# Zero-weight products with 64-row tiles and copies of dead banks, appended to the end of a one-core attention and feed-forward kernel

## The chip, the cores and the metric

The kernel runs on one core of a Trainium2 chip. The metric is device time in microseconds (us) of that core, the median of several executions. The profile is one more execution, in which the hardware profiler recorded every instruction of the core; its span runs from the first to the last instruction. PE is the matrix engine (PEld its weight loads), DVE the vector engine, ACT the scalar engine, POOL the third elementwise engine; SP issues most of the DMAs.

## What is computed

A gate mixes softmax attention with 32 heads of width 20 and a dense layer with the Mish activation, over 2048 rows of width 640. Cut to what matters:

```python
x = A_x                                             # [1, 2048, 640]
g = sigmoid((x * gate_w).sum(-1, keepdims=True))
q, k, v = split_heads(x @ A_wqkv)                   # 32 heads, 20 wide
a = concat_heads(softmax(q @ k.T * 20**-0.5) @ v) @ A_wo
h = x @ B_w1 + B_b1                                 # 1536 wide
b = (h * tanh(log1p(exp(h)))) @ B_w2
return g * a + (1 - g) * b
```

Both branches read the same input `A_x`. The appended work adds nothing to the output: it reads `xT` and a tile of zeros, writes accumulator banks whose last contents for the output have been read by then, and copies two of them to `accs`, which is not stored.

## The kernel before, in words

The accumulator memory `K.ps` has eight banks of 128 partitions x 512 float32. Banks 0 to 6 serve scores and dense products, bank 7 (`ACCB`) holds the sum of probabilities times values for one group of four heads and 512 queries. Every matrix product goes through the helper `mm` (L507), so one line stands for all of them; products that use a part of the array are told apart in the profile by a pair such as `128*32`, contraction rows times output columns:

- `32*128`, scores: each uses 32 rows of the array (one head, padded), and up to four with different rows run beside each other, each writing a bank of its own.
- `128*32`, values and dense layers: each uses 32 columns of the array. `mm4` (L512) issues four of them, for the four quarters of a bank's partitions; they run beside each other. Below, such a set of four is called a group. Some groups in the middle of the kernel have the tile of zeros, `K.zero`, as weights.

The order of all work was written down beforehand: a planner (`make_plan`) emits small functions, a stored list (`ORDER`) gives their order, and the last loop of the kernel calls them. Each engine then runs its own instructions strictly in that order; waits between engines are semaphores that the framework places where one instruction needs another's result. The last instructions of each engine are those of the output projection: on PE groups of 320 columns, on DVE `ost` (L751), on ACT `otmp` (L1218), on POOL the sum of the two (L1221), and on SP six stores of 128 rows each to the output (L452). Behind its last store SP waits for every DMA queue and every engine, and then the engines meet in a barrier (listed at the line of the last loop, L1801).

Lines that come up: L1394 and L1396 copy one half each (256 columns) of the last `ACCB` to `accs`, on DVE and on ACT; L1571 is a DVE copy on whose result PE's next weight load waits; L1753 are the 24 zero-weight products that open the program.

The banks in which PE's last groups ended, and that the output's last DVE and ACT instructions read, lie among 0 to 5; `ACCB` was read last near 735 us of the span.

Of the kernel before, what the change touches and what calls it, by code (L numbers as in the profile page):

```python
# [12 lines left out]
ACT = mybir.ActivationFunctionType  # L13
# [8 lines left out]
QC, NQC = 512, 4  # L22
# [6 lines left out]
NBANK, ACCB = 7, 7  # L29
# [232 lines left out]
def unpack(text):  # L262

    lo, out = 0, set()
    for k in range(0, len(text), 3):
        i = lo + int(text[k : k + 3], 16)
        yield i
        out.add(i)
        while lo in out:
            out.remove(lo)  # L270
            lo += 1
# [149 lines left out]

def make_plan(K, par):

# [25 lines left out]
    def ld(f):  # L449
        def fn():  # L450
            d, s = f()
            K.nc.sync.dma_start(out=d, in_=s)  # L452

        return fn

    def ldn(fs):
        def fn():
            for f in fs:
                d, s = f()
                K.nc.sync.dma_start(out=d, in_=s)  # L460

        return fn

    for (a, b), t in zip(XD, XAT):
        for i in range(a, b):
            pl.at(t, (lambda i=i: pl.give(("x", i))))
    pl.at(4300.0, lambda: act_q.append((460.0, (lambda: pad0(K.wk0, K.wkp)), (lambda: pl.give("wk0")))))
    pl.at(5600.0, lambda: act_q.append((460.0, (lambda: pad0(K.wq0, K.wqp)), (lambda: pl.give("wq0")))))
    pl.at(12200.0, lambda: pl.give("wv0"))
# [6 lines left out]
    def pad0(raw, dst):  # L476
        K.nc.scalar.activation(
            dst.rearrange("p k (r d) -> p k r d", r=4)[:, :, :, 0:DH], raw.rearrange("p k (r d) -> p k r d", r=4), ACT.Copy
        )
# [1172 lines left out]
    return dict(pl=pl, stat=stat, blk=blk, gtimes=gtimes, uinfo=uinfo)  # L1652


@with_exitstack
def kernel(
    ctx: ExitStack,
# [11 lines left out]
    nc = tc.nc  # L1669
    x2d = A_x[0]  # L1670
    K = Names()
    K.nc, K.A_wqkv, K.A_wo, K.B_w1, K.B_b1, K.B_w2 = nc, A_wqkv, A_wo, B_w1, B_b1, B_w2
    K.outp = out[0].rearrange("(p t) d -> t p d", t=NS)
    ctx.enter_context(tc.manual_schedule())
# [76 lines left out]
    for _ in range(NWARM):  # L1751
        for q in range(4):
            nc.tensor.matmul(  # L1753
                K.ps[32 * q : 32 * q + 32, ACCB, :],
                lhsT=K.zero,
                rhs=K.wkp.rearrange("p k c -> p (k c)")[:, 0:QC],
                start=True,
                stop=True,
                tile_position=(0, 32 * q),
                skip_group_check=True,  # L1760
# [12 lines left out]
    for i in unpack(ORDER):  # L1773
        for fn in plan["pl"].fns[i]:
            fn()


# [28 lines left out]
```

## Time and profile before

| what | us |
|---|---|
| executions | 746.64 and 747.2 |
| median | 746.92 |
| span of the profiled execution | 745.1 |
| busy: ACT / DVE / POOL | 713.2 / 607.1 / 521.9 |
| PE's share of the chain that ended last | 80% |

The profiled span is 1.8 us under the median of the timed executions. "Busy" is the time in which an engine had at least one instruction in flight. In a timeline each row is a run of equal instructions on one engine: the start, how long the run took, the engine, the line, what it writes and reads, and how many; a bracket says how long the engine had been idle and who released it. SPq, DVEq and the like are an engine's sequencer: its waits (EVENT_SEMAPHORE) and DMA issues. The granted clock of the matrix engine was 1.000 on average over the span.

### The profile page before, as it was taken

Reading aid. Unit: us, or ns where it says so; the run is one execution under the profiler, and the core shown is the slowest. Engines: PE = TensorE matmul, PEld = TensorE weight load, DVE = VectorE, ACT = ScalarE, POOL = GpSimd, SP = SyncE. Lnnn points to the kernel's source line nnn. Section 1 sums busy time; section 2 is a strip of 40 time slices with the busy share of each in tenths; the row PEclk is TensorE's granted clock in tenths of the full one; section 3 lists DMA queues with packets and bytes.
Section 4 is the critical chain, followed back from the end, with each engine's and each line's share of the span. In section 5 each row is a group of like instructions: output and inputs, shape, how many; then the busy total and the mean of one; then the engine's idle time right before and its main releaser. Section 6 shows DMA issues by size and latency. Waiting matters only on the chain.

```text
span 745.1 us, 24873 instructions
## 1 busy us (share of the span) xinstructions
PE 729.6 (98%) x10332; PEld 255.2 (34%) x10332; DVE 607.1 (81%) x1047; ACT 713.2 (96%) x750; POOL 521.9 (70%) x501
## 2 busy tenths in 40 slices
PE   8999999999999999999999999999999999999997
PEld 4433343333235333333332222223433333333333
DVE  4688888888979797988788878887878788797876
ACT  6899989999999999999999999999999999999995
POOL 9466735565578557667676587687986788797884
PEclk9999999999999999999999999999999999999999
DMA  9611120011011000112102211130111111211202
GB/s 284 199 48 54 50 82 17 20 52 39 17 29 60 16 29 26 50 44 74 39 28 59 54 43 50 39 101 21 43 52 39 39 38 39 71 60 60 72 21 86
DMA packets 45720, 41.82 MB, mean 56 GB/s; under 512 B 20120, under 2 KB 39240, under 8 KB 45608
## 3 DMA queue, kind: packets, MB, share of 16 engines
q1 hardware_dynamic: 42984, 39.94, 17.8%
q8 instruction: 80, 1.31, 0.7%
q10 hardware_dynamic: 2624, 0.31, 0.3%
q14 instruction: 32, 0.26, 0.1%
HBM read 27.59 MB, written 12.38 MB: 54 GB/s over the span
## 4 chain that ended last, share of the span: by engine, by line
PE 80%; ACT 10%; DVE 7%; issue 2%; POOL 0%; DVEq 0%; ACTq 0%; POOLq 0%
PE ps L507 80%; ACT E L1312 9%; DVE E L1347 4%; DVE E L1365 2%; DVE accs L1406 0%; POOL E L1365 0%; ACT act L1236 0%; PE ps L1753 0%; PE ps L520 0%; ACT xT L528 0%; ACT L1236 0%; DVE bst L656 0%; DVEq L1801 0%; DVE qT L544 0%; DVE ost L689 0%
## 5 line engine op out<-in xcount | busy, mean ns | idle before, releaser
L1312 ACT ACTIVATE E<-ps 128x1024 bf16<-128x1024 f32 (+2 forms) x723 | 680.0, 1070 | 19.3 <-PE ps L507 16.4
L1365 POOL TENSOR_SCALAR E<-E 128x1024 uint16<-128x1024 uint16 x431 | 457.8, 1063 | 209.7 <-DVE E L1347 155.0
L1347 DVE TENSOR_SCALAR E<-ps 128x512 uint16<-128x512 f32 x584 | 388.8, 684 | 94.1 <-PE ps L507 85.6
L507 PE MATMUL ps<-E,VA 128*32 128x512 bf16 x3216 | 299.4, 383 | 1.7 <-DVE E L1347 0.6
L507 PE MATMUL ps<-qT,kT 32*128 32x512 bf16 x2048 | 284.0, 384 | 5.3 <-ACT E L1312 2.6
L507 PEld LDWEIGHTS <-kT 32*128 32x128 bf16 x2048 | 75.3, 91 | 261.3 <-issue 257.2
L507 PEld LDWEIGHTS <-VA 128*32 128x32 bf16 x3216 | 78.9, 95 | 97.5 <-issue 78.2
L1365 DVE TENSOR_SCALAR E<-E 128x1024 uint16<-128x1024 uint16 x153 | 97.9, 643 | 2.0
L507 PE MATMUL ps<-R,act 128*32 128x320 bf16 x1536 | 87.1, 302 | 0.4 <-ACT act L1236 0.4
L507 PE MATMUL ps<-xT,R 128*32 128x512 bf16 x960 | 82.4, 383 | 0.0
L507 PEld LDWEIGHTS <-R 128*32 128x32 bf16 (+1 forms) x1728 | 40.8, 95 | 44.7 <-issue 34.0
L507 PEld LDWEIGHTS <-act 128*32 128x32 bf16 x1536 | 36.4, 95 | 32.1 <-issue 22.2
L637 DVE TENSOR_SCALAR act<-ps,b1f 128x512 bf16<-128x512 f32 x48 | 35.7, 744 | 7.4 <-PE ps L507 6.6
L507 PE MATMUL ps<-wv,xT 128*32 128x241 bf16 (+2 forms) x720 | 37.6, 276 | 0.5 <-DVE E L1347 0.3
L507 PE MATMUL ps<-wk,R 128*32 128x320 bf16 (+1 forms) x640 | 37.5, 303 | 0.2
L507 PE MATMUL ps<-xT,wq 128*32 128x512 bf16 x400 | 34.8, 383 | 0.1
L507 PE MATMUL ps<-xT,wk 128*32 128x512 bf16 (+1 forms) x360 | 34.7, 384 | 0.0
L1620 POOL TENSOR_TENSOR ons<-accs,rb 128x512 bf16<-128x512 f32 x24 | 31.5, 1310 | 1.8 <-DVE E L1347 0.7
L567 DVE CAST stg<-ps 128x512 bf16<-128x512 f32 (+1 forms) x40 | 27.3, 683 | 5.1 <-PE ps L507 4.9
L507 PEld LDWEIGHTS <-xT 128*32 128x32 bf16 (+1 forms) x720 | 19.6, 96 | 13.0 <-issue 9.4
L1406 DVE COPY accs<-ps 128x512 f32<-128x512 f32 x31 | 21.2, 684 | 1.3 <-PE ps L507 1.0
L1236 ACT ACTIVATE act<-act 128x3072 bf16<-128x3072 bf16 x8 | 21.5, 2752 | 0.0
(72 smaller groups left out, 190.3 us busy)
## 6 DMA issues: line engine op xcount, KB each, us to landing
rb<-rd_d SPq DMA_DIRECT2D x124, 64.0 KB
qd<-stg SPq DMA_DIRECT2D x20, 128.0 KB
b_d<-bst SPq DMA_DIRECT2D x16, 160.0 KB
out_dram<-ost SPq DMA_DIRECT2D x16, 160.0 KB
kT<-kd SPq DMA_DIRECT2D x28, 80.0 KB
qT<-qd SPq DMA_DIRECT2D x28, 80.0 KB
stg<-b_d SPq DMA_DIRECT2D x13, 160.0 KB
kd<-stg SPq DMA_DIRECT2D x16, 128.0 KB
```

Source lines behind the costliest of these rows:

```text
L507: K.nc.tensor.matmul(o, lhsT=l, rhs=r, start=first, stop=last, tile_position=pos, skip_group_check=True)
L567: K.nc.vector.tensor_copy(out=K.stg[0:w, s, :], in_=bank(b)[0:w, :])
L637: K.nc.vector.tensor_scalar(out=K.act[:, f, (c % 2) * QC : (c % 2 + 1) * QC], in0=bank(b), scalar1=K.b1f[:, f : f + 1], scalar2=None, op0= ...
L1236: K.nc.scalar.activation(a, a, ACT.Mish)
L1312: lambda: K.nc.scalar.activation(K.E[:, e : e + w, :], K.ps[:, b0 : b0 + w, :], ACT.Exp, scale=SCALE)
L1347: lambda: K.nc.vector.tensor_scalar(out=K.E[:, e + h, :].bitcast(U16), in0=K.ps[:, b, :], scalar1=CH_MUL, scalar2=CH_OFF + CH_ADD[0], op0= ...
L1365: eng.tensor_scalar(out=o, in0=i, scalar1=float(CH_ADD[k]), scalar2=1.0, op0=ALU.add, op1=ALU.mult)
L1406: emit(lambda: K.nc.vector.tensor_copy(out=K.accs[:, g % 2, :], in_=K.ps[:, ACCB, :]))
L1620: gp_q.append((1350.0, lambda: K.nc.gpsimd.tensor_tensor(out=dst(), in0=K.accs[:, b, :], in1=K.rb[:, b, :], op=ALU.mult), lambda: pl.give( ...
```

## The change

One function is added and called behind the loop that calls the planned functions, and a semaphore is allocated that nothing uses. The planned work and its order stay what they were on every engine.

`product` is one zero-weight product into a quarter of a bank. `full` is a group with all 128 rows of the array; `half(r, b)` is a group with 64 rows, the upper (`r` = 0) or the lower (`r` = 1), into bank `b`. `link` puts an empty instruction on an engine which waits for product `a`, and makes the products of list `b` wait for the empty instruction. `chain` writes the upper and the lower part of one sum into `ACCB` in turns, with a link at each turn and `more` pairs of half groups into other banks between the turns.

```diff
+def end_products(K):
+    dep = mybir.DependencyInfo(mybir.DependencyClass.Sync, mybir.DependencyReason.DATA)
+
+    def product(row, rows, col, b, n=QC, first=True, last=True):
+        return K.nc.tensor.matmul(
+            K.ps[32 * col : 32 * col + 32, b, 0:n],
+            lhsT=K.zero[row : row + rows, :],
+            rhs=K.xT[row : row + rows, 0, 0:n],
+            start=first,
+            stop=last,
+            tile_position=(row, 32 * col),
+            skip_group_check=True,
+        )
+
+    def full(b):
+        for q in range(4):
+            product(0, 128, q, b)
+
+    def half(r, b, n=QC, first=True, last=True):
+        return [product(64 * r, 64, q, b, n, first, last) for q in range(4)]
+
+    def link(eng, a, b):
+        n = eng.nop()
+        K.tc.add_manual_dep(n.ins, a.ins.name, dep, reason="row tiles in turn")
+        for i in b:
+            K.tc.add_manual_dep(i.ins, n.ins.name, dep, reason="row tiles in turn")
+
+    def chain(eng, more, b=None):
+        for k in range(4):
+            a = half(0, ACCB, first=True, last=False)
+            if b:
+                link(eng, b[-1], a)
+            for j in range(more):
+                half(0, (k + j) % 3)
+                half(1, 3 + (k + j) % 3)
+            b = half(1, ACCB, first=False, last=True)
+            link(eng, a[-1], b)
+            for j in range(more):
+                half(1, 3 + (k + j) % 3)
+                half(0, (k + j) % 3)
+        return b
+
+    full(ACCB)
+    full(ACCB)
+    b = chain(K.nc.sync, 1)
+    full(ACCB)
+    b = chain(K.nc.vector, 1, b)
+    full(ACCB)
+    chain(K.nc.sync, 2, b)
+    full(ACCB)
+    for _ in range(6):
+        half(0, 1)
+    half(1, 4)
+    K.nc.vector.tensor_copy(out=K.accs[:, 0, :], in_=K.ps[:, 4, :])
+    for _ in range(6):
+        half(0, 0)
+    full(ACCB)
+    for _ in range(6):
+        product(0, 64, 0, 0)
+    for q in range(1, 4):
+        product(0, 64, q, 0)
+    K.nc.vector.tensor_copy(out=K.accs[:, 1, :], in_=K.ps[:, 0, :])
+    full(ACCB)
+    full(ACCB)
+    for k in range(8):
+        if k >= 4:
+            K.nc.vector.nop()
+            K.nc.scalar.nop()
+        K.nc.vector.tensor_copy(out=K.accs[:, 0, 0:256], in_=K.ps[:, 0, 0:256])
+        K.nc.scalar.activation(K.accs[:, 1, :], K.ps[:, 1, :], ACT.Copy)
...
+    K.tc = tc
+    K.psem = tc.alloc_semaphore('psem')
...
         for fn in plan["pl"].fns[i]:
             fn()
+    end_products(K)
```

In the built program this is, behind the last instruction of each engine as it was: on PE 445 products, each with a weight load; on SP 15 empty instructions, behind its last store; on DVE 8 empty instructions and 10 copies; on ACT 8 copies. Each empty instruction is a wait for one count of PE's semaphore and an increment of a semaphore of its own; the first weight load of the linked group waits for that. The eight empty instructions of the last loop, which no dependency names, leave nothing in the program. Each of the eight DVE copies and the eight ACT copies of that loop waits for the one before it on its engine, since it overwrites the same part of `accs`; the first of ACT waits for the DVE copy into `accs[:, 1, :]`, and that one for the last of the nine products into bank 0. On PE two more waits are new: the first group into bank 3 waits for the last `ost` of DVE, and the first into bank 1 for the last `otmp` of ACT.

## The prediction

> **What bounds the end now.** Nothing moves before the appended work, so I read the end and the price of each piece. First the page's head, for the span against which the sum is made, and PE's load; next the timeline of the last microseconds, all engines, and with it the timeline from 733 us for SP's stores and the two accumulator copies.
>
> ```profile
> span 745.1 us, 24873 instructions
> PE 729.6 (98%) x10332; PEld 255.2 (34%) x10332; DVE 607.1 (81%) x1047; ACT 713.2 (96%) x750; POOL 521.9 (70%) x501
> ```
>
> ```profile
> 733.91 8.35 SPq L452 DMA_DIRECT2D out_dram<-ost  x6
> ...
> 734.34 0.43 DVE L1394 COPY accs<-ps 128x256 f32<-128x256 f32 x1 [0.45 <-PE ps L507]
> ...
> 734.80 0.38 ACT L1396 ACTIVATE accs<-ps 128x256 f32<-128x256 f32 x1 [1.16 <-DVE accs L1394]
> ```
>
> ```profile
> 740.33 0.32 PE L507 MATMUL ps<-wq,R 128*32 128x320 bf16 x4
> 740.33 0.53 ACT L1218 ACTIVATE otmp<-ps,gt 128x320 f32<-128x320 f32 x1 [1.58 <-PE ps L507]
> 740.40 1.47 DVE L751 SCALAR_TENSOR_TENSOR ost<-ps,gt,R 128x320 bf16<-128x320 f32 x3 [0.27 <-PE ps L507]
> 740.93 0.86 POOL L1221 TENSOR_TENSOR ost<-otmp,R 128x320 bf16<-128x320 f32 x1 [0.94 <-ACT otmp L1218]
> ```
>
> PE's last group starts at 740.33, DVE ends at 740.40 + 1.47 = 741.87, POOL at 741.79, SP issues its last store until 733.91 + 8.35 = 742.26. What follows to 745.1 is the landing of the stores and the closing barrier: 4.4 us in which PE does nothing. Appended work can hide there, and only there.
>
> Then prices. A stretch of PE's own timeline gives the step from group to group and what a change of the tile's form costs (first fence); a form-by-form list of ACT prices a copy (second); the timeline at 737.5 us (third) and the waits listed at two lines, count and shortest, median and longest ns (fourth), price a link.
>
> ```profile
> 722.28 0.60 PE L507 MATMUL ps<-E,VA 128*32 128x512 bf16 x8
> ...
> 724.84 0.31 PE L507 MATMUL ps<-wq,R 128*32 128x320 bf16 x4
> 725.08 0.39 PE L507 MATMUL ps<-qT,kT 32*128 32x512 bf16 x2
> 725.40 0.73 PE L507 MATMUL ps<-wk,R 128*32 128x320 bf16 x16
> ```
>
> ```profile
> L1312 ACT ACTIVATE E<-ps 128x1024 bf16<-128x1024 f32 x675 | 632.1, 1060 | 16.1 <-PE ps L507 13.4 <-POOL E L1365 0.5 <-ACT E L1312 0.3
> L1312 ACT ACTIVATE E<-ps 128x512 bf16<-128x512 f32 x15 | 9.4, 628 | 2.5 <-PE ps L507 2.4
> ```
>
> ```profile
> 737.50 0.29 DVE L1571 COPY R<-ps 128x256 bf16<-128x256 bf16 x1 [0.72 <-PE ps L1564]
> ...
> 737.85 0.12 PEld L507 LDWEIGHTS <-R 128*32 128x32 bf16 x8 [0.26 <-DVE R L1571]
> ```
>
> ```profile
> L452 SPq EVENT_SEMAPHORE  x26: 17/17/2224, 250.0 to 741.8; - x26
> ...
> L751 DVEq EVENT_SEMAPHORE  x4: 21/21/21, 737.5 to 740.4; - x4
> ```
>
> Readings. Two groups of 512 columns took 0.60 us where one takes 0.38: a step T = 0.22. Sixteen products of 320 columns took 0.73, so (0.73 - 0.31) / 3 = 0.14 a group, 34 ns a product with its weight load. From the 320-column group at 724.84 to the scores at 725.08 it is 0.24 instead of 0.14, and from the scores to the next form 0.32 instead of 0.22: a change of form costs s = 0.10. After the DVE copy ended at 737.79, PE's dependent load began at 737.85: 0.05 from engine to PE. PE's groups that ran from 739.91 for 0.44 ended at 740.35, and DVE began at 740.40: again 0.05. An empty wait takes 17 to 21 ns.
>
> **The sum, piece by piece.** A link starts at the end of a half group X, 0.39 after X's start (0.38 and the stagger of four), crosses to SP or DVE (0.05), waits there 0.02, crosses back (0.05): the linked group Y starts 0.51, with rounding 0.52, after X. In between PE streams one half group on X's side and one on the other. Four scores of different rows, into four banks, take 0.40 us in this trace (at 724.15), as long as one, so I take upper and lower half groups as running beside each other too: X and the pair need 2T = 0.44. The link ends last: P1 = 0.52 a turn. With `more` = 2 it is 3T = 0.66, over 0.52: the link is hidden and P2 = 0.66; if pairs ran faster, the link's 0.52 would be next late. `half` has a form of its own (64 rows), and the nearest row for its change is s = 0.10, between 128 and 32 rows; from below it is 0.
>
> The start: two full groups at 740.47 and 740.69, the first half group into `ACCB` at 741.01 (0.22 + s), bank 0 at 741.23. The group into bank 3 waits for DVE's 741.87. The first Y waits for SP's empty instruction, which stands behind the last store: 742.26 + 0.05 (issue to next, as SP does now) + 0.02 + 0.05, so 742.38. SP has nothing behind that but the other links and the closing waits; the store itself is not delayed. On DVE the links stand behind the last `ost`, and ahead of copies that need PE anyway. The waits for bank 1 (ACT, over at 740.86) and the landing stores cost nothing.
>
> - First chain: 6 more turns, 742.38 + 6 x 0.52 = 745.50. A step to the last pair, the full group after T + s, the next chain after T + s again: 0.22 + 0.32 + 0.32 brings it to 746.36.
> - Second chain, links on DVE: 7 x 0.52 + 0.86 = 4.50: 750.86.
> - Third chain: 7 x 0.66 + 2 x 0.22 + 0.32 + 0.32 = 5.70: 756.56.
> - Twelve half groups on one side, 12 x 0.22 = 2.64 (the one into bank 4 runs beside the sixth, and its DVE copy, 0.68 by the 512-column copies at L1406, hides under the next six): 759.20. Full group with two changes of form, 0.42: 759.62.
> - Six products on one and the same tile follow each other: the sixth starts 5 x 0.22 later, 760.72, the other three quarters beside it, end 761.12. The last two full groups, 0.6 us, hide under what follows.
> - The DVE copy of bank 0: 0.05 + 0.68, 761.85. From here the two engines run eight copies each. DVE: 0.43 by L1394, and 0.03 between an instruction and the next that needs it (L1554 behind L1553 at 735.99), 8 x 0.46 = 3.7. ACT: 256 columns took 0.38 and from 512 to 1024 it is (1060 - 628) / 2 = 216 ns per 256 columns, so 0.60, and 0.04 between dependent ones (an ACT instruction that waited for the one just before it began 43 ns behind it, at 630.5 us): 8 x 0.64 = 5.12. ACT ends last: 761.90 + 5.12 = 767.02. The eight empty instructions that would stand between copies are not in the program: nothing.
> - The closing: SP's last waits started at 743.84 and the span ended at 745.1, so 1.26 after its last wait; 0.03 to get there: 768.3.
>
> That is 23.2 us over 745.1. The profiled execution lies 1.8 under the median, and I let that stand: 746.92 + 23.2 = 770.1.
>
> **Bounds.** Below: a hidden link gives P1 = 0.44, 13 turns x 0.08 = 1.0; no cost of the form's change, eight on the path, 0.8; copies overlapping by 0.13, as ACT's independent instructions do (0.93 apart at 1.06 each), 8 x 0.17 = 1.3. Together 767.0. Above: a link dearer by 0.2 costs 13 x 0.2 and 7 x 0.06, 3.0: 773.1. The Trainium skill's page "TensorE: Matmul & The Clock Gate", section "The cost: per-tile semaphore tail", gives a formula for the time behind the last product, 70 ns for four tiles and one increment, an estimate where the trace has 50; by it the 13 binding links would cost 0.3 us more.
>
> **Rivals.**
>
> 1. *Upper and lower run one after the other.* The trace never shows 64-row tiles, nor eight tiles at once, only four. Then X and the pair take 3T = 0.66, with `more` = 2 five T = 1.10: 13 x 0.14 + 7 x 0.44 + about 1.1 for pairs at the chains' ends and the group into bank 4, 6.0: 776.1. For it: nothing but the absence of a row. Against: four row tiles of the scores together take 0.32 to the next form, as three do. 0.12.
> 2. *Links dearer by 0.2 or more*, an engine's sequencer slower to answer PE than to answer DVE: 773 to 776. Against: 17 and 21 ns waits at both. 0.06.
> 3. *A price per product at issue.* A P1 turn has 12 products, so it decides from 43 ns each, P2 from 33. The densest long rows show 34: P2 0.68, 0.1 us in all. The dearest row of short products is that of 128x80 at full array width, 4.8 us busy for 80, 60 ns each with their filling: P1 0.72, P2 1.20, 13 x 0.20 + 7 x 0.54 = 6.4, 776.5. Against: the 34 ns hold at the end of the kernel, over 16 products. 0.02. The Trainium skill's "TensorE: Matmul & The Clock Gate", section "Step-by-step: what each phase is for", has 62 ns a product where the sequencer decodes products in its firmware; by that rule, as an estimate, it would be 777, and the 34 ns measured here disagree with it.
> 4. *The clock falls.* The opening zero-weight products took 627 ns where later ones take 382. If the gaps of the chains lowered the clock, steps double: about 15 us, 785. Against: PE's longest gap would be some 0.8 us, at the start, and by the view of waits PE waited as long for ACT (L528) before; the mean granted clock was still 1.000. 0.03.
> 5. *Not slower.* The two halves share one accumulator bank; if a link did not hold PE's queue, and groups of the other side passed it, the three chains would be 44 pairs, 9.7 us, where I have 0.52 x 16 + 0.66 x 8 = 13.6. It decides where the whole addition falls to 14.9 us (2% of 746.92). Taking off 3.9, the lower bounds that this doesn't contain (0.8 and 1.3) and the wait at the start (0.9) leaves 16.3, 763.2; to reach 761.8 ACT's copies have to take 0.30 besides, where half their columns took 0.38. Against: each engine goes through its waits in order everywhere in this trace. 0.02.
>
> **The numbers.** The forecast itself, 767 to 773 around 770.1, has 0.75. The range takes in rival 1 and most of 2 and 3: 767 to 776.5. A measurement of this kernel tells 2% from no change, 14.9 us, and all cases but rival 5 lie over it: slower 0.97, within 2% 0.02, faster 0.01.
>
> **What would show it.** Right: in the trace after, turns of 0.52 us in the first two chains and 0.66 in the third; PE's last product near 761.5; eight ACT copies 0.64 apart and nothing after them but 1.3 us of barrier; all rows before 740 as they were. Wrong: lower half groups that start when upper ones end (rival 1); an idle gap on PE at each turn of the third chain too (2); 627-ns products (4). What would upset the sum most is a wait that I have not seen in the program's order: PE's queue held up by a load that waits while products behind it could run.

## The result

The changed kernel took 770.92 us, the median of 768.97 and 772.87, against 746.92 before: 1.0315 times as long, 95% interval 1.0248 to 1.0382. Forecast were 770.1 us and a range of 767.0 to 776.5. A second series, told below, gave 769.46 (six executions) against 746.86 (eleven), 1.0295 with an interval of 1.0264 to 1.0326.

The head of the page after:

```profile
span 771.0 us, 25807 instructions
...
PE 750.8 (97%) x10777; PEld 263.4 (34%) x10777; DVE 610.4 (79%) x1057; ACT 717.8 (93%) x758; POOL 522.1 (68%) x501
```

All 445 added products, 10 DVE copies and 8 ACT copies are there. But the span grew by 25.9 us, and not all of that is the change: this one execution was late before it came to the addition. The timeline of PE after shows where (start, length, engine, line, what, idle before):

```profile
5.47 1.28 PE L520 MATMUL ps<-ident,act 128*128 128x128 bf16 x10 [0.20 <-DMA act<-in_A_x_dram]
10.07 2.32 PE L507 MATMUL ps<-xT,wkp 128*32 128x512 bf16 x20 [3.32 <-ACT xT L528]
...
744.10 0.32 PE L507 MATMUL ps<-wq,R 128*32 128x320 bf16 x4
```

The same projection before, by PE's timeline:

```profile
7.23 1.26 PE L507 MATMUL ps<-xT,wkp 128*32 128x512 bf16 x20 [0.79 <-ACT xT L528]
```

PE waited 3.32 us for its first projection, and the granted clock averaged 0.81 between 7 and 16 us, where it had been 1.00 before; twenty products that had taken 1.26 us took 2.32. PE came to its last group of the output projection at 744.10 instead of 740.33. The next section tells whether this belongs to the change. The addition itself is read from that group on:

| from the start of PE's last projection group, us | forecast | after |
|---|---|---|
| first half group | 0.68 | 0.68 |
| first linked half group | 2.05 | 2.05 |
| second chain begins | 6.03 | 5.94 |
| third chain begins | 10.53 | 10.50 |
| the twelve half groups on one side begin | 16.23 | 15.33 |
| DVE copy of bank 0 | 20.84 | 19.89 |
| first ACT copy | 21.57 | 20.61 |
| last ACT copy ends | 26.69 | 25.61 |
| end of the span (before: 4.77) | 27.97 | 26.90 |

So the addition is 26.90 - 4.77 = 22.1 us, where 23.2 were forecast. One step is off by 0.9 us: from the beginning of the third chain to the twelve half groups it is 4.83 us, where 5.70 were forecast. The timeline of the weight loads shows the turns, since each linked group begins with a load that waits. First two turns linked by SP, then two by DVE, then the third chain:

```profile
746.15 0.13 PEld L1660 LDWEIGHTS <-zero 64*32 64x32 bf16 x12 [0.35 <-SPq L1678]
746.65 0.13 PEld L1660 LDWEIGHTS <-zero 64*32 64x32 bf16 x12 [0.37 <-SPq L1678]
...
750.57 0.13 PEld L1660 LDWEIGHTS <-zero 64*32 64x32 bf16 x12 [0.40 <-DVEq L1678]
751.09 0.13 PEld L1660 LDWEIGHTS <-zero 64*32 64x32 bf16 x12 [0.40 <-DVEq L1678]
...
755.10 0.33 PEld L1660 LDWEIGHTS <-zero 64*32 64x32 bf16 x20 [0.17 <-SPq L1678]
755.61 0.40 PEld L1660 LDWEIGHTS <-zero 64*32 64x32 bf16 x20 [0.17 <-SPq L1678]
756.18 0.33 PEld L1660 LDWEIGHTS <-zero 64*32 64x32 bf16 x20 [0.17 <-SPq L1678]
```

The turns are 0.50 us (SP) and 0.53 (DVE), forecast 0.52; but in the third chain 0.51 and 0.57 in turns, 0.54 on average, where the forecast had 0.66. The end of the chain of waits shows the rest, one copy after the other (start, length, what):

```profile
746.15 17.82 PE ps L1660 x414
763.97 0.02 issue
763.99 0.70 DVE accs L1717
764.69 0.02 issue
764.71 0.61 ACT accs L1725
765.32 0.02 issue
765.34 0.61 ACT accs L1725
...
769.11 0.60 ACT accs L1725
```

### The profile page after: what moved, and what is told of

It reads as the page before. It is cut to its first block, busy times and chain, and to the rows that moved or that the text cites. A ratio compares the mean times of both kernels' runs of the same rounds, so it can differ in the third digit from the quotient of the medians.

```text
span 771.0 us, 25807 instructions
## 1 busy us (share of the span) xinstructions
PE 750.8 (97%) x10777; PEld 263.4 (34%) x10777; DVE 610.4 (79%) x1057; ACT 717.8 (93%) x758; POOL 522.1 (68%) x501
## 4 chain that ended last, share of the span: by engine, by line
PE 80%; ACT 10%; DVE 7%; issue 2%; DMA 1%; POOL 0%; ACTq 0%; SPq 0%; DVEq 0%; POOLq 0%
PE ps L507 78%; ACT E L1312 8%; DVE E L1347 3%; PE ps L1660 2%; DVE E L1365 2%; DMA wq<-in_A_wqkv_dram 1%; ACT accs L1725 1%; DVE accs L1406 0%; POOL E L1365 0%; ACT act L1236 0%; ACT L1236 0%; DVE ost L751 0%; DVE bst L656 0%; DVE accs L1717 0%; DVE qT L544 0%
## 5 line engine op out<-in xcount | busy, mean ns | idle before, releaser
L1725 ACT ACTIVATE accs<-ps 128x512 f32<-128x512 f32 x8 | 4.8, 597 | 20.3 <-DVE accs L1717 20.1
```

Source lines behind the costliest of these rows:

```text
L1725: K.nc.scalar.activation(K.accs[:, 1, :], K.ps[:, 1, :], ACT.Copy)
```

## The experiments

My theory after this reading: the sum is right but for one step, that PE starts products strictly in the order of the program. Its rival keeps that order and looks for the 0.9 us elsewhere. T is the 0.216 us from group to group on one tile row.

**The same kernel again.** No edit.

> The changed kernel once more, five rounds. From PE's last product of the output projection to the end the first profile has 26.9 us, and 4.8 before, so the addition is 22.1 us and executions should lie at 746.9 + 22.1 = 769.0. The profiled execution was 3.8 us later already at the output projection. Theory 'chance': that comes from the order in which the first loads land, is no part of the change, and only some executions have it: most executions near 769.0, some near 772.9. Rival 'part of the change': every execution of the longer program starts late, all within 771 to 773.

Six executions: 768.46, 768.9, 769.28, 769.64, 769.8 and 771.92; median 769.46. Five lie within 0.8 us of 769.0 and one is late. The profiled one reached the last projection group at 740.51, and the seven other experiments, all with work added behind the same program, reached it between 739.67 and 741.56. The late start is no part of the change; it is in one of the first two executions, which is why their median is 0.8 us above the forecast though the addition was smaller. Its way is in the chain of waits of the first profile: the load of `wq` was issued at 1.22 us as in the other profiles, but ACT's copy of it, for which ACT's copy of `xT` and so PE had to wait, began at 8.89, where it began between 5.83 and 6.96 in the nine other profiles. Why the load was late is not shown. The kernel before has a late execution as well, one of its eleven with 753.35 us; that one and the 771.92 were not profiled, so whether they were late in the same way stays open.

In this profile the stretch from PE's last projection group to the end took 27.35 instead of 26.90, and the timeline shows the 0.45:

```profile
741.63 1.27 SPq L452 DMA_DIRECT2D out_dram<-ost  x2
...
743.00 0.13 PEld L1660 LDWEIGHTS <-zero 64*32 64x32 bf16 x12 [0.79 <-SPq L1678]
```

SP issued its last two stores until 742.90, 2.39 us after PE's last projection group at 740.51, instead of 1.94; the first linked group follows at 743.00. The first link does stand behind SP's stores.

**The copies left out.**

```diff
-    for k in range(8):
...
-        K.nc.vector.tensor_copy(out=K.accs[:, 0, 0:256], in_=K.ps[:, 0, 0:256])
-        K.nc.scalar.activation(K.accs[:, 1, :], K.ps[:, 1, :], ACT.Copy)
```

> Leaves out the last loop, the eight DVE and eight ACT copies. If they stand alone at the end, as the sum has it, the end comes with the DVE copy of bank 0, 0.68 us after PE's count: the stretch from PE's last product of the output projection to the end falls from 26.9 by 5.0 to 21.9 us, the time by 5.0 to about 764. Rival: the copies' place is taken by something else that ends late (the last two groups, the closing waits), and less than 4 us is gained.

764.39 us, 5.07 less than the 769.46; 1.0223 of before, interval 1.0191 to 1.0255. The stretch was 22.35, 5.00 less than the 27.35 of the run above; in both a last store took SP long to issue (0.74 and 0.79 us). The copies stand alone at the end, as the sum had it.

**The links left out.** The lower half groups write bank 6, so nothing has to be kept apart.

```diff
-            a = half(0, ACCB, first=True, last=False)
-            if b:
-                link(eng, b[-1], a)
+            a = half(0, ACCB)
...
-            b = half(1, ACCB, first=False, last=True)
-            link(eng, a[-1], b)
+            b = half(1, 6)
```

> The lower half groups of the chains write bank 6 instead of the shared bank, and the 23 empty instructions with their waits are gone; the same products stay. Theory 'passing' (a product whose tile is free starts ahead of older products that wait for another tile): both sides of the array stay full, a turn of three groups takes 1.5 T = 0.32 us instead of 0.50 (SP) and 0.53 (VectorE), the third chain stays at 2.5 T = 0.54; the addition falls by 8 x 0.18 + 8 x 0.20 + about 0.3 at the start = 3.3 us. Theory 'strict order' (of my prediction): a turn takes 2 T = 0.43, the addition falls by about 1.5 us.

766.67 us (four executions), 2.8 less than the 769.46. The loads of the three chains in its timeline:

```profile
743.16 2.27 PEld L1660 LDWEIGHTS <-zero 64*32 64x32 bf16 x87 [0.80 <-issue]
745.86 0.10 PEld L1660 LDWEIGHTS <-zero 128*32 128x32 bf16 x4 [0.43 <-issue]
746.19 2.30 PEld L1660 LDWEIGHTS <-zero 64*32 64x32 bf16 x96 [0.23 <-issue]
748.92 0.10 PEld L1660 LDWEIGHTS <-zero 128*32 128x32 bf16 x4 [0.42 <-issue]
749.25 4.03 PEld L1660 LDWEIGHTS <-zero 64*32 64x32 bf16 x160 [0.23 <-issue]
753.70 0.10 PEld L1660 LDWEIGHTS <-zero 128*32 128x32 bf16 x4 [0.43 <-issue]
```

From one full group's loads to the next, 745.86 to 748.92, is 3.06 us for the second chain's 24 half groups and the full group with two changes of form. That is (3.06 - 0.43) / 24 = 0.110 a half group, half of T: the two sides are both full. In strict order it would have been 8 x 0.43 + 0.43 = 3.9 and more. The third chain takes 753.70 - 748.92 = 4.78, and with the links it took 759.10 - 754.27 = 4.83: the links cost it 0.05 in all. From the last projection group to the twelve half groups it is 12.47 us (754.03 less 741.56), 2.86 less than the 15.33 of the first profile; "passing" had 3.3, "strict order" 1.5. Most of what "passing" had too much is in the first chain: its twelve lower groups all come after the wait for DVE's last `ost`, at 743.16 to 745.53, so one side alone takes 12 T there.

**How far a product passes.** Sets of n groups on one tile and one on another.

```diff
-    b = chain(K.nc.sync, 1)
...
+    for n in (1, 2, 3, 4, 6, 8, 12):
+        for _ in range(n):
+            half(0, 1)
+        half(1, 4)
+        full(ACCB)
...
+            product(0, 128, 0, 0)
+        product(0, 128, 1, 0)
```

> Instead of the appended work: n upper half groups on one tile row and then one lower half group, with n = 1, 2, 3, 4, 6, 8, 12, each set closed by a full group; then n products on one column quarter and one on the next quarter, with n = 3, 6, 12, 24, for 64 rows and for 128. No empty instructions and no copies. Theory 'passing': the last one of each set starts ahead of the older ones, up to some number of instructions, and each set with small n ends as if it weren't there: n T plus the changes of form. Theory 'strict order': the last one starts when the last older one has started, never before. Where passing ends tells how far PE looks ahead; in the changed kernel it went past three groups.

One execution, 776.2 us. These are the starts of the groups in ns from the first of their set, in the order of the records; the start that doesn't fit the steps of 216 is the other tile's:

```
n     starts                                                              next full group
1     0, 13                                                               339
2     0, 27, 227                                                          542
3     0, 40, 227, 443                                                     759
4     0, 53, 227, 442, 658                                                974
6     0, 227, 443, 459, 659, 874, 1090                                    1406
8     0, 227, 443, 658, 874, 890, 1090, 1306, 1522                        1838
12    0, 226, 442, 658, 874, 1090, 1305, 1521, 1737, 1753, 1953, 2169, 2385   2700
```

Up to n = 4 the odd group starts at once. From n = 6 on it starts with the (n - 3)th, so three older groups always start later. Single products on one column quarter do the same: of 24 with 64 rows the odd one starts after the 21st, at 4333 ns, and of 24 with 128 rows at 4322. Every set lasts n T and 0.11 to 0.12 us for the change of form; the odd group adds nothing.

That the odd one really is the younger one, one record shows by itself. In the changed kernel's six upper groups and one lower, the one product that increments PE's semaphore is the last of the lower group; its record starts at 759.900 us, and upper groups that stand before it in the program start at 760.090, 760.306 and 760.522. The increment was seen only at 760.970.

**The lower group first.**

```diff
+    half(1, 4)
     for _ in range(6):
         half(0, 1)
-    half(1, 4)
```

> The lower half group into bank 4 is issued ahead of the six upper ones instead of behind them. Theory 'counts in order': PE's semaphore counts products in the program's order, also where one finished ahead of older ones; the bank's copy on VectorE then starts about 0.45 us after the block's first product instead of 1.64, and the end stays (26.9 to 27.4 us from PE's last product of the output projection). Rival 'counts as they finish': in the changed kernel the copy would have been let go at 0.9; it was not, so a copy that again starts at 1.6 would leave the cause of that wait open.

Its timeline:

```profile
755.62 1.43 PEld L1660 LDWEIGHTS <-zero 64*32 64x32 bf16 x36 [0.23 <-issue]
756.14 0.69 DVE L1709 COPY accs<-ps 128x512 f32<-128x512 f32 x1 [14.30 <-PE ps L1660]
```

The bank's copy starts 0.52 us after the block's first load, and 761.07 - 759.43 = 1.64 in the changed kernel, though there the lower group had run its 0.39 us by 760.29. Here the lower group ended at 756.02 and PE's count came at 756.05; in the changed kernel it came at 760.97, just after the last of the older groups had ended at 760.91. So the count goes in the program's order, and a product that passed others is not seen to be finished before them. The stretch stayed at 26.92; the time was 768.99 (one execution, with 745.88 before in the same series).

**Patterns on two sides.** Half groups alone, without links or copies.

```diff
+    for u, l in ((12, 2), (12, 4), (12, 8)):
+        for _ in range(u):
+            half(0, 1)
+        for _ in range(l):
+            half(1, 4)
+        full(ACCB)
...
+        for _ in range(8):
+            half(0, 1)
+        for _ in range(8):
+            half(1, 4)
```

> Only half groups on the two row tiles, without links and copies: 12 upper then 2, 4 or 8 lower; upper, upper, lower, lower six times; upper, lower six times; four and four, three times; eight and eight, three times. Theory 'three wait per tile' (a product passes older ones while no more than three of them wait for another tile): with T = 0.216 the first lower group of the 12 + 8 set starts with the ninth upper one, the set takes 16 T; four and four three times takes 12 T; eight and eight three times 28 T. Theory 'strict order': 19 T, 19 T and 43 T. A window counted in instructions over all tiles would let lower groups pass in four and four only where fewer than some 12 products wait.

One execution, 768.7 us. From the set's first group to the full group behind it, less 0.12 us for the change of form: twelve and eight 3.59 - 0.12 = 16.1 T, the first lower one starting with the ninth upper one at 1753 ns; four and four 2.945 - 0.12 = 13.1 T; eight and eight 6.667 - 0.12 = 30.3 T. Strict order, 19, 19 and 43, is out. Twelve and two took 12.0 T and twelve and four 12.1, where strict order gives 13 and 15; the sets that change sides after one group or two took 6.0 and 12.1 T, where it gives 6 and 13. Three waiting ones per tile explain the first exactly; for the two that change sides often they give 12 and 28, some 8% too little, so that rule is not the whole of it, and what else limits the passing stays open.

**Other engines for the link.** Four chains with one pair between turns; what follows them is left out.

```diff
-    b = chain(K.nc.sync, 1)
+    b = chain(K.nc.vector, 1)
     full(ACCB)
-    b = chain(K.nc.vector, 1, b)
+    b = chain(K.nc.sync, 1, b)
     full(ACCB)
-    chain(K.nc.sync, 2, b)
+    b = chain(K.nc.gpsimd, 1, b)
     full(ACCB)
+    chain(K.nc.scalar, 1, b)
```

> Only chains of one pair between turns, linked by empty instructions of VectorE, SyncE, GpSimd and ScalarE in turn; the rest of the appended work and the copies are left out. Theory 'crossing': a turn is a half group's 0.39 us plus the way to the engine and back, so 0.53 on VectorE and 0.50 on SyncE wherever the chain stands, and 0.50 to 0.55 on the other two. Rival 'place': the first chain is the quicker, 0.50, whatever engine. The first link on VectorE doesn't stand behind SyncE's stores: the first linked group should come 1.7 us after PE's last product of the output projection, instead of 2.05 (2.5 where a store took longer to issue).

One execution, 762.28 us. Its timeline, two turns for each engine:

```profile
743.72 0.13 PEld L1660 LDWEIGHTS <-zero 64*32 64x32 bf16 x12 [0.40 <-DVEq L1678]
744.25 0.13 PEld L1660 LDWEIGHTS <-zero 64*32 64x32 bf16 x12 [0.40 <-DVEq L1678]
...
747.68 0.13 PEld L1660 LDWEIGHTS <-zero 64*32 64x32 bf16 x12 [0.37 <-SPq L1678]
748.18 0.13 PEld L1660 LDWEIGHTS <-zero 64*32 64x32 bf16 x12 [0.37 <-SPq L1678]
...
752.12 0.13 PEld L1660 LDWEIGHTS <-zero 64*32 64x32 bf16 x12 [0.39 <-POOLq L1678]
752.64 0.13 PEld L1660 LDWEIGHTS <-zero 64*32 64x32 bf16 x12 [0.39 <-POOLq L1678]
...
756.62 0.13 PEld L1660 LDWEIGHTS <-zero 64*32 64x32 bf16 x12 [0.39 <-ACTq L1678]
757.13 0.13 PEld L1660 LDWEIGHTS <-zero 64*32 64x32 bf16 x12 [0.38 <-ACTq L1678]
```

0.53, 0.50, 0.52 and 0.51 us: it goes by the engine and not by the place, and the engines hardly differ. The first link ran on DVE at 741.46, long before SP's last store. But the first linked group, told by its product that increments PE's semaphore, started at 742.14, 1.82 us after the last projection group, where 1.7 was expected: it waited for the lower group ahead of it, which had waited for DVE's last `ost` until 741.93. Meanwhile, at 741.97, the upper group behind the linked one had started ahead of it.

**Copies that don't wait for each other.** ACT's copies go to `accs` and to `otmp` in turns.

```diff
-        K.nc.scalar.activation(K.accs[:, 1, :], K.ps[:, 1, :], ACT.Copy)
+        o = K.otmp.rearrange("p t c -> p (t c)")[:, 0:QC] if k % 2 else K.accs[:, 1, :]
+        K.nc.scalar.activation(o, K.ps[:, 1, :], ACT.Copy)
```

> ScalarE's eight copies write accs and the dead otmp in turns, so that each waits for the one before the last instead of the last. Theory 'own result': the 0.63 us from copy to copy is the copy's whole length and a wait; without the wait the copies overlap as the exponentials do, 0.48 apart, the last stage falls by 7 x 0.15 = 1.0 us. Rival 'rate': 0.63 is what 512 columns cost on ScalarE, and nothing changes.

```profile
760.75 0.60 ACT L1726 ACTIVATE accs<-ps 128x512 f32<-128x512 f32 x1 [20.07 <-DVE accs L1717]
761.25 0.59 ACT L1726 ACTIVATE otmp<-ps 128x512 f32<-128x512 f32 x1
761.73 0.60 ACT L1726 ACTIVATE accs<-ps 128x512 f32<-128x512 f32 x1
...
764.11 0.67 ACT L1726 ACTIVATE otmp<-ps 128x512 f32<-128x512 f32 x1
```

The timeline has the copies 0.48 us apart, (764.11 - 760.75) / 7, instead of 0.63; the stretch fell from 26.90 to 25.93. A copy takes as long as before or a little longer, 0.59 to 0.67, but the next one begins inside it. So the 0.63 was the wait for the last result, not ACT's rate. The time was 767.85 (one execution, with 745.88 before in the same series).

## Why the prediction was right, and where it was not

- **The start.** Right to 0.01 us: two full groups, the change of form, the wait for DVE's last `ost`, and the first link behind SP's last store. What the sum took as fixed is not: an issue on SP can take longer, and then the link waits 0.4 more (`again`).
- **Links, P1.** Forecast 0.52, measured 0.50 on SP and 0.53 on DVE. The price of a turn was right, and what bounds it too: without links a turn falls to 1.5 T. The 2T I gave as what would be late next was wrong, for the reason in the next point; as the link ended later, that cost the sum nothing.
- **The third chain, P2.** This is the step that failed. "With `more` = 2 it is 3T = 0.66, over 0.52: the link is hidden and P2 = 0.66." The link is hidden, but PE does not start the groups in the order of the program: I let a group whose own side was free wait for an older group of the other side. PE starts it ahead, both sides stay full, and five groups take 2.5 T = 0.54. Eight turns at 0.12 less are the 0.9 us that the table shows.
- **Rival 1, sides one after the other,** is out: a half group takes half of T where both sides have work.
- **Rival 2, dearer links,** and **rival 3, a price at issue,** are out as well: turns as forecast, and 20 products in 0.54 us, 27 ns each. The 62 ns a product of the Trainium skill's "TensorE: Matmul & The Clock Gate", section "Step-by-step: what each phase is for", where they are decoded in firmware, are not what bounds products here.
- **Rival 4, the clock,** did not touch the addition, but the opening of one execution. In the first profile the granted clock was 0.50 between 10.1 and 13.4 us, after PE had waited 3.32 us, which is longer than any wait in the chains; from 744.1 to 767.8, past PE's last product, it was 1.00.
- **Rival 5, passing,** had a true mechanism with a wrong reach: products do pass older ones that wait for a tile, but not one that waits for a semaphore. In the first chain the upper group behind the first linked one stood still until 746.18 though its tile had been free since about 745.2; it started 0.03 us after the linked group. In `four_engines`, where that link had been served long before, the same upper group started 0.17 us ahead of the linked one.
- **Change of form.** 0.10 to 0.11 from 128 to 64 rows and back (groups 0.330 and 0.316 apart instead of 0.216), forecast 0.10 from the 32-row neighbour.
- **Copies and closing.** 5.00 for 5.12, and 1.29 from the last copy to the end for 1.28.
- **The time.** 746.92 + 22.1 = 769.0 is where most executions of the second series lie. That the 770.92 is nearer to the forecast than the addition is, is luck: the late start of one execution makes up for the third chain. Without it the time is still inside the range.

## What to carry to other kernels

Work appended behind a kernel can hide in the time between the old last product and the old end, here 4.8 us; what goes beyond that is read from the longest of its own queues, turn by turn. When two row or column tiles share PE, count each tile's own queue, not the order of issue, as long as no product between them waits for a semaphore and only a few wait for their tile; put a product whose result is wanted early also early in the program, since it is counted in order. Let ACT's copies in a row write different places, and don't hang a link on a queue that still has DMAs to issue.

## What the hardware did that I had not expected

- A product starts ahead of older products that wait for their tile, with up to three of these left behind in the sets with one odd group or product; row tiles of 64 rows and column tiles of 64 and 128 rows all did so. The Trainium skill's page "TensorE: Matmul & The Clock Gate", section "The mechanism", says that products start and end strictly in program order; the start at 759.900 ahead of those at 760.090 to 760.522 contradicts it for starts, and the count at 760.970 agrees with it as far as what other engines see. The words ahead of the prediction, that each engine runs its instructions strictly in the order of the program, are wrong for the starts of PE's products in the same way.
- The empty instruction's round trip hardly depends on the engine: turns of 0.50 (SP), 0.51 (ACT), 0.52 (POOL) and 0.53 us (DVE).
- One of the last two stores took SP 0.73 to 1.13 us to issue in the four profiles of one series (`again`, `no_copies`, `no_links`, `depth`), and 0.33 in the six others. `again` and the first profile have the same program, so the program alone is not the cause; what is stays open.
